# Attention, layer norm and feed-forward on one core: the first batch's weights rounded with one VectorE shift, sign and last bits made on ScalarE, differences on VectorE

## The chip, the cores and the metric

The kernel runs on one core of one Trainium2 chip. The metric is the device time of one launch in microseconds (us). Engines are called by the profile's names: PE (TensorE products), PEld (its weight loads), DVE (VectorE), ACT (ScalarE), POOL (GpSimd) and SP (SyncE, which here only issues transfers).

## The reference, cut to what matters

Four batches of causal attention (12 heads, 448 positions, head size 64), then a layer norm with gain and a feed-forward block with a residual. Shapes: `q`, `k`, `v` are (4, 12, 448, 64), the weights are 768 x 3072 and 3072 x 768.

```python
scores = scale * np.matmul(q, k.transpose(0, 1, 3, 2))   # masked above the diagonal
attn = softmax(scores)                                   # rows, max subtracted
x = np.matmul(attn, v)                                   # -> (4, 448, 768)
xn = (x - mu) / np.sqrt(var + 1e-06) * g_ln
out = x + np.maximum(xn @ w_ch1, 0.0) @ w_ch2
```

The scales in the set-up turn the inputs, the weights too, into float64, so a weight reaches the chip as two 32-bit words.

## The kernel before, in words

**Slots.** The feed-forward work of a batch is cut into 48 slots of 18 matrix products. Two slots use one weight unit of 128 x 1536, so a slot uses one half unit of 128 x 768. Slots 0 to 47 are batch 0, 48 to 95 batch 1, and so on. In each half of a batch 12 slots are products with `w1` (tile `ph`, L416) and 12 with `w2` (tile `po`, L435). Every float32 factor is split into two float32r parts whose sum it is: weights into `wh` and `wl`, activations into `xh`, `xl` and `hh`, `hl`. A product of 128 x 128 by 128 x 448 is three matmuls: high by high, low by high, high by low.

**Attention beside it.** While a batch's slots run, the attention of the next batch is worked on between them: one pair of heads in six slots, called a pair period here. Batch 0's own attention runs before slot 0, in slots with negative numbers (from about -50), with nothing beside it but the first four half units; batch 1's first pair of heads has its scores there too. The scores (`sc`, L229) get their mask and row minimum on DVE (L237), their exponentials on ACT (L251) and their scaling by `norm` (L267, tile `P` or `rest`), on POOL in batch 0 and on DVE in later batches; then PE transposes them (`pt`, L283), ACT or DVE evicts that (`PT`, L286 or L288), and PE multiplies by `v` (`px`, L298). In later batches DVE and POOL also make the parts of `q` and `k` (`qs` L195, `kl` L198).

**A half unit of the first batch.** `load_raw` brings in the float64 words (tile `raw`, five buffers), one slot's 128 x 768 at a time. Before the change, four instructions make the float32 weight, and two more split it:

- `convert1`: POOL multiplies the high word, read as a float32, by 0.0 and by 1.0 (L93, tile `z`: a zero with the weight's sign); ACT multiplies the same word by 2^-112 (L96, tile `w`), which puts the exponent where three shifts to the left make it float32's.
- `convert2`: DVE shifts the low word right by 29 and sets the sign bit into it (L101, `z`), then shifts `w` left by 3 and sets `z` into it (L105). The bits below float32's last place are cut off.
- `keep`: SP stores `w` in DRAM (L111, `scratch`), from where the three other batches load it (`full`).
- `split1`: ACT copies `w` to float32r (L116, `wh`); `split2`: `wl = w - wh` (L121), on POOL in the first batch, on DVE in the others.

**What sets the order.** Everything is issued in an order written out by the program, and each engine works through its own instructions in that order. In a slot first come the attention steps in `pre`, then the weight steps of `weights_ahead` (sorted: `split2`, `convert2`, `convert1`, `keep`, `load_raw`, `load_full`, `split1`), then the 18 products with their evictions (`hh` on ACT, L421, and `hl` on DVE, L422, or `xT` on DVE, L439), then the attention steps in `post`. From half unit 4 on, half unit s has `convert1` in slot s-4, `convert2` in s-3, `split1` in s-2 and `split2` in s-1. Half units 0 to 3 have them in the slots before 0, six slots apart.

Of the kernel before, what the change touches and what calls it, by code (L numbers as in the profile page):

```python
# [8 lines left out]
F32 = mybir.dt.float32  # L9
F32R = mybir.dt.float32r  # L10
U32 = mybir.dt.uint32
ACTF = mybir.ActivationFunctionType
ALU = mybir.AluOpType
PSUM = bass.MemoryType.PSUM
DRAM = bass.MemoryType.DRAM
# [4 lines left out]
P = 128  # L20
# [7 lines left out]
UH = UE // 2  # L28
# [11 lines left out]
ELAG = [2, 5, 7]  # L40
NDVE = 7
STATS = [(0, 3), (3, 5), (5, 6)]
OFF = [C * (i * (i + 1) // 2) for i in range(NC + 1)]


@with_exitstack
def kernel(ctx, tc, qk, v, w1, w2, g, out):
    nc = tc.nc

    def pool(name, bufs, **kw):  # L50
        return ctx.enter_context(tc.tile_pool(name=name, bufs=bufs, **kw))

    const = pool("const", 1)
    sb = pool("sb", 1)
# [5 lines left out]
    g_sb = const.tile([P, KC], F32, name="g_sb")  # L60
    mhalf = const.tile([C, NC], F32, name="mhalf")

# [1 line left out]
    # The first batch takes each unit from its float64 words, rounds it to float32 on the chip and  # L64
    # leaves it in DRAM for the other batches; every batch splits a unit into two float32r parts
    # whose sum is the float32.
    order = []
    for f0, f1 in ((0, HF), (HF, NF)):
        order += [("w1", f // 2) for f in range(f0, f1, 2)]
# [1 line left out]
    ns = 2 * len(order)  # L71
    scratch = [dr.tile([P, UE], F32, name=f"scratch{i}") for i in range(len(order))]
    ready = set()
    raw, zs, w32, wh, wl = {}, {}, {}, {}, {}

    def load_raw(s):
        kind, i = order[s // 2]
# [6 lines left out]
    def load_full(s):  # L84
        t = sb.tile([P, UE], F32, tag="raw", name="full", bufs=5)
        nc.sync.dma_start(out=t, in_=scratch[s % ns // 2])
        w32[s], w32[s + 1] = t[:, :UH], t[:, UH:]

    def convert1(s):
        high = raw[s][:, :, 1].bitcast(F32)  # L90
        zs[s] = sb.tile([P, UH], F32, tag="z", name="z", bufs=3)
        w32[s] = sb.tile([P, UH], F32, tag="w32", name="w32", bufs=4)
        nc.gpsimd.tensor_scalar(  # L93
            out=zs[s], in0=high, scalar1=0.0, scalar2=1.0, op0=ALU.mult, op1=ALU.mult
        )
        nc.scalar.activation(out=w32[s], in_=high, func=ACTF.Copy, scale=2.0 ** -112)  # L96

    def convert2(s):
        ready.add(s)
        z, w = zs.pop(s).bitcast(U32), w32[s].bitcast(U32)  # L100
        nc.vector.scalar_tensor_tensor(  # L101
            out=z, in0=raw.pop(s)[:, :, 0], scalar=29, in1=z,
            op0=ALU.logical_shift_right, op1=ALU.bitwise_or,
        )
        nc.vector.scalar_tensor_tensor(  # L105
            out=w, in0=w, scalar=3, in1=z, op0=ALU.logical_shift_left, op1=ALU.bitwise_or
        )

    def keep(s):
# [7 lines left out]

    def split2(s):
        wl[s] = sb.tile([P, UH], F32R, tag="wl", name="wl", bufs=4)
        eng = nc.gpsimd if s < ns else nc.vector  # L120
        eng.tensor_tensor(  # L121
            out=wl[s], in0=w32[s], in1=wh[s].bitcast(F32), op=ALU.subtract
        )

    def weights_ahead(start):
        """By slots, the work on the weights of later slots; the first halves of units are made
        ready while the first batch's attention runs."""
        early = 4
        todo = {}

        def put(t, *fs):
            todo.setdefault(max(t, start), []).extend(fs)

        for s in range(B * ns):
            t = (-EARLY + GAP * s, *ELAG) if s < early else (s - 4, 1, 2, 3)
            put(t[0] + t[3], (split2, s))
            if s < ns:
                put(t[0], (convert1, s))
                put(t[0] + t[1], (convert2, s))
                put(t[0] + t[1] + 1, (keep, s))  # L140
                if s + 5 < ns:
                    put(t[0] + t[1] + 1, (load_raw, s + 5))
            elif s % 2 == 0:
                put(s - 8, (load_full, s))
            put(t[0] + t[2], (split1, s))
        rank = [split2, convert2, convert1, keep, load_raw, load_full, split1]
        for fs in todo.values():
            fs.sort(key=lambda f: rank.index(f[0]))
        return todo

# [1 line left out]
    class Att:  # L152
        def __init__(self, b):
            self.b = b
# [45 lines left out]
        def scores(self, p, grp):  # L200
# [8 lines left out]
            for h, i in grp:  # L209
                n = C * (i + 1)  # L210
                if ("P", p, h) not in self.t:
                    x = 2 * p + h
                    if self.b == 0 and x % 5 >= 3:
                        a = 2 * NC * D * NP + (x % 5 - 3) * OFF[NC]
                        old = (x - 5) // 2, (x - 5) % 2
                        assert x < 5 or all(("T", *old, j) in self.done for j in range(NC))
                        self.t["P", p, h] = rest[:C, a:a + OFF[NC]]
                    else:
                        self.t["P", p, h] = sb.tile([C, OFF[NC]], F32, tag="P", name="P", bufs=3)
                if self.b == 0:  # L220
# [14 lines left out]
            for x, (h, i) in enumerate(grp):  # L235
                n = C * (i + 1)
                nc.vector.tensor_tensor_reduce(  # L237
                    out=self.t["P", p, h][:, OFF[i]:OFF[i + 1]], in0=pt[:, o:o + n],
                    in1=mask[:, S - n:], op0=ALU.add, op1=ALU.min, scale=-0.125, scalar=3.0e38,
# [5 lines left out]
        def exps(self, p, grp):  # L245
            nm = self.t.pop(("nm", p, tuple(grp)))
            for x, (h, i) in enumerate(grp):
                if ("sm", p, h) not in self.t:
                    self.t["sm", p, h] = sb.tile([C, NC], F32, tag="sm", name="sm", bufs=6)
                pp = self.t["P", p, h][:, OFF[i]:OFF[i + 1]]  # L250
                nc.scalar.activation(  # L251
# [5 lines left out]
        def norm(self, p, h):  # L257
# [7 lines left out]
            for i in (0, 1, 3, 2):  # L265
                pp = self.t["P", p, h][:, OFF[i]:OFF[i + 1]]
                eng.tensor_scalar(  # L267
# [37 lines left out]
        def stats(self, part, x):  # L305
            c0, c1 = STATS[part]
            assert all(("pv", c) in self.done for c in range(c0, c1))
            self.done.add(("stats", part, x))
            pt = ps.tile([C, S], F32, tag="pt", name="pln")
            for c in range(c0, c1):  # L310
                nc.tensor.transpose(  # L311
                    pt[:, (c - c0) * P:(c - c0 + 1) * P], self.xT[:, c, x * C:(x + 1) * C], ident
                )
            nc.vector.bn_stats(out=self.stat[:, x, part, :], in_=pt[:, :(c1 - c0) * P])
# [44 lines left out]
            )  # L359

        def steps(self):
            """The work by slots, relative to the first pair's: what goes before the products of
            the feed-forward layers in a slot, and what goes behind them."""
            pre, post = {}, {}

            def put(where, t, f, *a):
                where.setdefault(t, []).append((f, a))

            if self.b == 0:
                sat, tat, nat, end, ev = SAT0, TAT0, NAT0, END0, EV0  # L370
            else:
                sat, tat, nat, end, ev = SAT, TAT, NAT, END, EV1 if self.b == 1 else EV
            period = 6
            for p in range(NP):
                t0 = period * p
                if self.b:
                    put(pre, t0 - 4, self.load, p)
                    put(pre, t0 - 2, self.split1, p)
                    put(pre, t0 - 1, self.split2, p)
                for h in range(2):  # L380
                    put(pre, t0 + nat[h], self.norm, p, h)
                put(post, t0 + end, self.pv, p)
                for x, grp in enumerate(TGROUPS):
                    put(post, t0 + tat[x], self.transposes, p, grp, "act" if ev[x] else "dve")
                for x, grp in enumerate(SGROUPS):
                    put(post, t0 + sat[x], self.scores, p, grp)
                    put(pre, t0 + sat[x] + 1, self.exps, p, grp)
            tl = period * (NP - 1) + end + 1
            th = TH0 if self.b == 0 else TH
            for x in range(NC):  # L390
                put(post, th[0] + x, self.stats, 0, x)
                put(post, th[1] + x, self.stats, 1, x)
                put(post, tl + x // 2, self.stats, 2, x)
            ta = tl + NC // 2
            put(pre, ta, self.aggr)
            put(post, ta, self.spread)
            for c in range(KC):
                x = c if self.b else c // 2
                put(pre, ta + 1 + x, self.apply1, c)
                put(pre, ta + 1 + x + (self.b > 0), self.apply2, c)  # L400
            return pre, post, ta + (7 if self.b else 4)

# [1 line left out]
    def ffn(a, s, hh, hl):  # L404
        for f0, f1 in ((0, HF), (HF, NF)):
            for x in range(0, HF, 2):
# [38 lines left out]
    with tc.manual_schedule():  # L445
# [23 lines left out]
        for p in range(NP):  # L469
# [7 lines left out]
            out=mask[:, S - C:], in_=mask[:, S - C:], compare_op=ALU.is_ge, fill=-8.0e9,  # L477
# [3 lines left out]
        for s in range(4, 5):  # L481
            pre.setdefault(start + 6 + 4 * s, []).append((load_raw, (s,)))
        feed, ahead = None, weights_ahead(start)
        for s in range(start, B * ns):
            for b in range(1, B):
# [6 lines left out]
            if s >= 0:  # L492
# [3 lines left out]
                if s % ns == 0:  # L496
                    feed = ffn(att[s // ns], s, hh, hl)
# [38 lines left out]
```

## Time and profile before

| what | value |
|---|---|
| median of 3 runs | 960.81 us (958.25 to 961.01) |
| span of the profiled execution | 955.6 us |
| that execution's own time | not listed apart from its span; the median is 5.2 us above the span |
| PE busy | 908.6 us (95%) |
| PEld busy | 794.1 us (83%) |
| DVE busy | 626.7 us (66%) |
| ACT busy | 416.8 us (44%) |
| POOL busy | 283.1 us (30%) |

The span runs from the first to the last instruction. Busy time is the time in which an engine works at least on one instruction; an instruction that is held up by another engine counts as busy as long as it is held. Percentages are means over stages that differ, so the stages are looked at one by one below.

### The profile page before, as it was taken

What the parts mean: (1) busy time and instruction counts of PE and PEld (TensorE: products, weight loads), DVE (VectorE), ACT (ScalarE), POOL (GpSimd) and SP (SyncE); (2) the same over time, 40 slices, a digit from 0 to 9 for tenths busy, and PEclk for the clock granted to TensorE, in tenths of its full rate; (3) what the DMA queues carried; (4) which work ended last, traced back from release to release, by engine and by line L of the source; (5) the groups of instructions that cost most, each with busy time, mean ns of one, the idle gap of its engine ahead of it and who ended that gap; (6) DMA issues with size and microseconds to landing.
All of it is one profiled execution on the core that took longest, in us unless ns stands there. A gap on an engine that the chain in (4) does not pass through costs nothing.

```text
span 955.6 us, 13000 instructions
## 1 busy us (share of the span) xinstructions
PE 908.6 (95%) x4864; PEld 794.1 (83%) x4864; DVE 626.7 (66%) x1208; ACT 416.8 (44%) x859; POOL 283.1 (30%) x211
## 2 busy tenths in 40 slices
PE   6888988998998799999999999999999999999998
PEld 4556877887787698898888998898888999999997
DVE  5978999999989746656565566666665544333432
ACT  6754565547553344444543245443443233323320
POOL 7654675887758901111010311110010210000000
PEclk9988998999999999999999999999999999999999
DMA  9730667767677654332322463323322243233310
GB/s 252 270 112 1 213 232 270 250 221 278 217 249 239 234 192 147 115 135 80 134 80 76 150 226 115 139 87 137 115 100 76 98 165 116 100 103 119 108 56 36
DMA packets 35246, 144.36 MB, mean 151 GB/s; under 512 B 4080, under 2 KB 8688, under 8 KB 35184
## 3 DMA queue, kind: packets, MB, share of 16 engines
q1 hardware_dynamic: 35184, 143.54, 43.5%
q8 instruction: 38, 0.62, 0.3%
q14 instruction: 24, 0.20, 0.1%
HBM read 119.15 MB, written 24.38 MB: 150 GB/s over the span
## 4 chain that ended last, share of the span: by engine, by line
PE 65%; POOL 0%; DVE 0%; ACT 0%; issue 0%; POOLq 0%; ACTq 0%
PE po L435 29%; PE ph L416 28%; PE sc L229 3%; PE px L298 3%; PE pt L283 2%; PE pln L311 1%; POOL wl L121 0%; PE rb L336 0%; PE mb L331 0%; DVE w L105 0%; ACT wh L116 0%; DVE xT L439 0%; POOL xl L356 0%; POOLq L121 0%; ACTq L116 0%
## 5 line engine op out<-in xcount | busy, mean ns | idle before, releaser
L435 PE MATMUL po<-hh,wl 128*128 128x448 f32 x576 | 212.7, 369 | 8.7 <-POOL wl L121 8.7
L416 PE MATMUL ph<-xh,wh 128*128 128x448 f32 x576 | 215.2, 374 | 3.4 <-DVE hl L422 2.0
L435 PE MATMUL po<-hh,wh 128*128 128x448 f32 x576 | 215.6, 374 | 0.0
L416 PE MATMUL ph<-xl,wh 128*128 128x448 f32 x576 | 212.1, 368 | 0.5 <-POOL xl L356 0.5
L416 PE MATMUL ph<-xh,wl 128*128 128x448 f32 x576 | 211.4, 367 | 1.0 <-POOL wl L121 1.0
L435 PE MATMUL po<-hl,wh 128*128 128x448 f32 x576 | 212.0, 368 | 0.0
L422 DVE SCALAR_TENSOR_TENSOR hl<-ph,hh 128x448 fp32r<-128x448 f32 x96 | 59.7, 622 | 128.1 <-ACT hh L421 128.1
L116 ACT ACTIVATE wh<-full 128x768 fp32r<-128x768 f32 x144 | 119.5, 839 | 54.8 <-PE po L435 50.8
L121 DVE TENSOR_TENSOR wl<-full,wh 128x768 fp32r<-128x768 f32 x144 | 136.3, 953 | 0.8 <-ACT wh L116 0.5
L198 POOL TENSOR_TENSOR kl<-qkraw,kh 128x896 fp32r<-128x896 f32 x18 | 48.2, 2678 | 278.8 <-DVE kh L188 267.3
L251 ACT ACTIVATE P<-P,nm 112x448 f32<-112x448 f32 (+3 forms) x176 | 91.7, 522 | 81.9 <-DVE nm L237 77.9
L435 PEld LDWEIGHTS po<-hh,wl 128*128 128x128 f32 x576 | 109.2, 190 | 20.4 <-POOL wl L121 11.6
L421 ACT ACTIVATE hh<-ph 128x448 fp32r<-128x448 f32 x96 | 51.9, 540 | 162.8 <-PE ph L416 162.7
L416 PEld LDWEIGHTS ph<-xh,wh 128*128 128x128 f32 x576 | 109.2, 190 | 13.0 <-DVE hl L422 2.3
L416 PEld LDWEIGHTS ph<-xh,wl 128*128 128x128 f32 x576 | 108.9, 189 | 10.3 <-POOL wl L121 1.7
L435 PEld LDWEIGHTS po<-hh,wh 128*128 128x128 f32 x576 | 109.4, 190 | 8.5
L416 PEld LDWEIGHTS ph<-xl,wh 128*128 128x128 f32 x576 | 109.1, 189 | 8.8 <-POOL xl L356 0.9
L435 PEld LDWEIGHTS po<-hl,wh 128*128 128x128 f32 x576 | 109.3, 190 | 8.2
L121 POOL TENSOR_TENSOR wl<-w,wh 128x768 fp32r<-128x768 f32 x48 | 103.2, 2151 | 36.8 <-issue 15.2
L439 DVE TENSOR_TENSOR xT<-po,xT 128x448 f32<-128x448 f32 x48 | 29.9, 622 | 115.6 <-PE po L435 115.6
L237 DVE CUSTOM_DVE_ANT_0 P<-sc,mask 112x448 f32<-112x448 f32 (+3 forms) x176 | 70.2, 443 | 38.2 <-PE sc L229 26.6
L105 DVE SCALAR_TENSOR_TENSOR w<-w,z 128x768 uint32<-128x768 uint32 x48 | 90.0, 1875 | 3.1
(64 smaller groups left out, 1049.0 us busy)
## 6 DMA issues: line engine op xcount, KB each, us to landing
full<-scratch SPq DMA_DIRECT2D x72, 768.0 KB, 4.2
raw<-w_dram SPq DMA_DIRECT2D x48, 768.0 KB, 4.9
scratch<-w SPq DMA_DIRECT2D x48, 384.0 KB, 2.7
qkraw<-qk_dram SPq DMA_DIRECT2D x18, 896.0 KB, 7.2
out_dram<-xT SPq DMA_DIRECT2D x24, 224.0 KB, 2.0
vt<-v_dram SPq DMA_DIRECT2D x18, 224.0 KB, 5.6
first_qk<-qk_dram SPq DMA_DIRECT2D x8, 224.0 KB, 5.3
rest<-v_dram SPq DMA_DIRECT2D x6, 224.0 KB, 7.4
```

Of the source, the lines that this page charges most:

```text
L105: nc.vector.scalar_tensor_tensor(out=w, in0=w, scalar=3, in1=z, op0=ALU.logical_shift_left, op1=ALU.bitwise_or)
L116: nc.scalar.activation(out=wh[s], in_=w32[s], func=ACTF.Copy)
L121: eng.tensor_tensor(out=wl[s], in0=w32[s], in1=wh[s].bitcast(F32), op=ALU.subtract)
L198: nc.gpsimd.tensor_tensor(out=kl, in0=rk, in1=kh.bitcast(F32), op=ALU.subtract)
L229: nc.tensor.matmul(pt[:, o:o + n], lhsT=qs[:, h, C * i:C * i + C], rhs=kk[:, h, :n], start=(part == 0), stop=(part == 1),)
L237: nc.vector.tensor_tensor_reduce(out=self.t["P", p, h][:, OFF[i]:OFF[i + 1]], in0=pt[:, o:o + n], in1=mask[:, S - n:], op0=ALU.add, op1=AL ...
L251: nc.scalar.activation(out=pp, in_=pp, func=ACTF.Exp, scale=-1.0, bias=nm[:, x:x + 1], accum_out=self.t["sm", p, h][:, i:i + 1],)
L416: nc.tensor.matmul(pm[y], lhsT=w[:, c * P:c * P + P], rhs=z[:, c, :], start=(c == 0 and i == 0), stop=(c == KC - 1 and i == 2),)
L421: nc.scalar.activation(out=hh[:, x + y, :], in_=pm[y], func=ACTF.Relu)
L422: nc.vector.scalar_tensor_tensor(out=hl[:, x + y, :], in0=pm[y], scalar=0.0, in1=hh[:, x + y, :].bitcast(F32), op0=ALU.max, op1=ALU.subtract,)
L435: nc.tensor.matmul(pm, lhsT=w[:, o:o + P], rhs=z[:, x, :], start=(x == 0 and i == 0), stop=(x == HF - 1 and i == 2),)
L439: nc.vector.tensor_tensor(out=a.xT[:, m, :], in0=pm, in1=a.xT[:, m, :], op=ALU.add)
```

## The change: what it does, and the diff

The sign no longer has a tile of its own. ACT's multiplication becomes a two-sided one (Prelu): a positive high word is multiplied by 2^-112, a negative one by 2^-80, which sets the bit that the shift by three moves into the sign's place. A second ACT instruction turns the low word, a whole number, into the last bits: times 239/256 x 2^-29, converted to a whole number (tile `bits`), which rounds where the shift cut off. DVE is left with one instruction, the shift of `w` with `bits` set into it. `split2` is on DVE in the first batch too. POOL has no weight work any more.

```diff
+LAST = 239 / 256
...
     def convert1(s):
-        high = raw[s][:, :, 1].bitcast(F32)
-        zs[s] = sb.tile([P, UH], F32, tag="z", name="z", bufs=3)
+        bits[s] = sb.tile([P, UH], U32, tag="bits", name="bits", bufs=3)
         w32[s] = sb.tile([P, UH], F32, tag="w32", name="w32", bufs=4)
-        nc.gpsimd.tensor_scalar(
-            out=zs[s], in0=high, scalar1=0.0, scalar2=1.0, op0=ALU.mult, op1=ALU.mult
+        nc.scalar.activation(
+            out=w32[s], in_=raw[s][:, :, 1].bitcast(F32), func=ACTF.Prelu, scale=2.0 ** -112,
+            alpha=2.0 ** 32,
         )
-        nc.scalar.activation(out=w32[s], in_=high, func=ACTF.Copy, scale=2.0 ** -112)
+        nc.scalar.activation(
+            out=bits[s], in_=raw.pop(s)[:, :, 0], func=ACTF.Copy, scale=LAST * 2.0 ** -29
+        )
...
     def convert2(s):
         ready.add(s)
-        z, w = zs.pop(s).bitcast(U32), w32[s].bitcast(U32)
+        w = w32[s].bitcast(U32)
         nc.vector.scalar_tensor_tensor(
-            out=z, in0=raw.pop(s)[:, :, 0], scalar=29, in1=z,
-            op0=ALU.logical_shift_right, op1=ALU.bitwise_or,
-        )
-        nc.vector.scalar_tensor_tensor(
-            out=w, in0=w, scalar=3, in1=z, op0=ALU.logical_shift_left, op1=ALU.bitwise_or
+            out=w, in0=w, scalar=3, in1=bits.pop(s), op0=ALU.logical_shift_left,
+            op1=ALU.bitwise_or,
         )
...
     def split2(s):
         wl[s] = sb.tile([P, UH], F32R, tag="wl", name="wl", bufs=4)
-        eng = nc.gpsimd if s < ns else nc.vector
-        eng.tensor_tensor(
+        nc.vector.tensor_tensor(
             out=wl[s], in0=w32[s], in1=wh[s].bitcast(F32), op=ALU.subtract
         )
```

**DVE, in a pair period of batch 0's slots, before.** The rows go from the end of one slot (its eviction `hl`) over the scaling of a head and the copy `kh` to the next slot's eviction. The numbers behind `w` are the half unit's.

```order
L422 SCALAR_TENSOR_TENSOR hl<-ph,hh 128x448
L262 TENSOR_SCALAR r<-sm 112x4
L263 RECIPROCAL r<-r 112x4
L267 TENSOR_SCALAR P<-P,r 112x112
...
L188 CAST kh<-qkraw 128x896
L101 SCALAR_TENSOR_TENSOR z<-raw,z 128x768
L105 SCALAR_TENSOR_TENSOR w_1293<-w_1293,z 128x768
L422 SCALAR_TENSOR_TENSOR hl<-ph,hh 128x448
L195 TENSOR_TENSOR qs<-qkraw,qs 64x896
```

The same stretch of the changed program:

```order
L427 SCALAR_TENSOR_TENSOR hl<-ph,hh 128x448
L267 TENSOR_SCALAR r<-sm 112x4
L268 RECIPROCAL r<-r 112x4
L272 TENSOR_SCALAR P<-P,r 112x112
...
L193 CAST kh<-qkraw 128x896
L126 TENSOR_TENSOR wl<-w_1177,wh 128x768
L110 SCALAR_TENSOR_TENSOR w_1282<-w_1282,bits 128x768
L427 SCALAR_TENSOR_TENSOR hl<-ph,hh 128x448
L200 TENSOR_TENSOR qs<-qkraw,qs 64x896
```

DVE still has two weight instructions in a slot: the shift that made `z` has gone, and in its place, one earlier, stands the difference `wl` of the half unit two steps ahead in its making.

**ACT, the same pair period's end, before and in the changed program** (`P,sm` are the exponentials, `PT` the evicted transposes):

```order
L251 ACTIVATE P,sm<-P,nm 112x112
L251 ACTIVATE P,sm<-P,nm 112x336
L96 ACTIVATE w_1610<-raw 128x768
L116 ACTIVATE wh<-w_1506 128x768
L286 COPY PT<-pt 112x448
```

```order
L256 ACTIVATE P,sm<-P,nm 112x112
L256 ACTIVATE P,sm<-P,nm 112x336
L99 ACTIVATE w_1593<-raw 128x768
L103 ACTIVATE bits<-raw 128x768
L122 ACTIVATE wh<-w_1491 128x768
L291 COPY PT<-pt 112x448
```

One instruction more stands between the exponentials and `wh`. In both programs ACT has one table load, at its beginning.

**POOL, at the first slots of batch 0, before and in the changed program** (`xl` belongs to the layer norm of batch 0, `kl` to batch 1's heads):

```order
L356 TENSOR_TENSOR xl<-xg,xh 128x448 x6
L93 TENSOR_SCALAR z<-raw 128x768 x3
L198 TENSOR_TENSOR kl<-qkraw,kh 128x896
L121 TENSOR_TENSOR wl<-w_939,wh 128x768
L93 TENSOR_SCALAR z<-raw 128x768
```

```order
L361 TENSOR_TENSOR xl<-xg,xh 128x448 x6
L203 TENSOR_TENSOR kl<-qkraw,kh 128x896
```

Behind it, POOL's next instruction in the changed program is the `kl` of the next pair of heads. The orders of PE and of SP are the same in both programs.

## Rows read from the trace of the kernel before

**Rows 1.** The page's busy tenths in 40 slices of the span.

```profile
PE   6888988998998799999999999999999999999998
DVE  5978999999989746656565566666665544333432
```

**Rows 2.** Busy time by stage: slots 0 to 47, slots 48 to 95, one pair period.

```profile
core 0: us, PE busy (x) PEld busy (x) DVE busy (x) ACT busy (x) POOL busy (x), PEclk, DMA share, GB/s
84.20:339.70 255.50, 230.05 (x1201) 198.81 (x1202) 233.80 (x325) 134.90 (x252) 190.07 (x107) 0.96 0.66 228
339.70:558.10 218.40, 218.40 (x1218) 195.62 (x1217) 133.86 (x311) 92.75 (x198) 25.29 (x13) 1.00 0.36 125
...
114.60:148.10 33.50, 30.81 (x169) 26.32 (x168) 31.39 (x50) 20.18 (x41) 24.23 (x14) 1.00 0.70 246
```

**Rows 3.** The chain that ended last: start, duration, what.

```profile
324.84 2.49 POOL wl L121
327.37 12.36 PE po L435 x52
...
347.05 0.91 PE sc L229 x6
...
351.62 0.81 PE sc L229 x6
...
356.08 0.51 PE sc L229 x4
...
375.24 1.10 PE sc L229 x6
```

**Rows 4.** PE's waits, 84 to 340 us: total, times, longest.

```profile
PE pt L283 <- DVE P L267: 13.1, 11, 2.5
PE po L435 <- POOL wl L121: 8.7, 7, 1.9
```

**Rows 5.** DVE in order of time: start, duration.

```profile
207.70 2.42 DVE L105 SCALAR_TENSOR_TENSOR w<-w,z 128x768 uint32<-128x768 uint32 x1
```

**Rows 6.** POOL over the same stretch, 199 to 214 us.

```profile
206.76 2.54 POOL L121 TENSOR_TENSOR wl<-w,wh 128x768 fp32r<-128x768 f32 x1
```

**Rows 7.** Durations by tile, ns: least, median, most.

```profile
L101 DVE SCALAR_TENSOR_TENSOR z<-raw,z x48: 935/1122/4452, 15.3 to 324.3; 128x768 uint32<-128x768 uint32 x48
L105 DVE SCALAR_TENSOR_TENSOR w<-w,z x48: 957/1625/6049, 16.5 to 325.7; 128x768 uint32<-128x768 uint32 x48
L121 DVE TENSOR_TENSOR wl<-full,wh x144: 941/950/1336, 333.8 to 945.2; 128x768 fp32r<-128x768 f32 x144
L96 ACT ACTIVATE w<-raw x48: 869/899/933, 14.3 to 320.4; 128x768 f32<-128x768 f32 x48
L198 POOL TENSOR_TENSOR kl<-qkraw,kh x18: 2067/2712/2786, 54.8 to 696.9; 128x896 fp32r<-128x896 f32 x18
L195 DVE TENSOR_TENSOR qs<-qkraw,qs x18: 1089/1242/4120, 53.7 to 699.3; 64x896 fp32r<-64x896 f32 x18
```

**Rows 8.** DVE's groups in the pair period: busy us, mean ns, idle before.

```profile
L105 DVE SCALAR_TENSOR_TENSOR w<-w,z 128x768 uint32<-128x768 uint32 x6 | 12.2, 2028 | 0.2
L101 DVE SCALAR_TENSOR_TENSOR z<-raw,z 128x768 uint32<-128x768 uint32 x6 | 7.0, 1169 | 0.0
```

**Rows 9.** DVE and POOL before slot 0, each in order of time.

```profile
23.01 4.45 DVE L101 SCALAR_TENSOR_TENSOR z<-raw,z 128x768 uint32<-128x768 uint32 x1
...
22.93 1.95 POOL L267 TENSOR_SCALAR rest<-rest,r 112x112 f32<-112x112 f32 x4
24.80 1.84 POOL L121 TENSOR_TENSOR wl<-w,wh 128x768 fp32r<-128x768 f32 x1
```

**Rows 10.** PE's waits over the whole span.

```profile
PE pt L283 <- DVE PT L288: 6.4, 3, 3.0
```

**Rows 11.** Groups of the whole span: xl on POOL, the table load on ACT.

```profile
L356 POOL TENSOR_TENSOR xl<-xg,xh 128x448 fp32r<-128x448 f32 x24 | 32.2, 1341 | 39.1 <-ACT xh L353 38.7
...
L251 ACT ACT_TABLE_LOAD x1 | 1.3, 1283 | 0.7 <-PEq L525 0.7
```

More of the change, by code (lines that the diff above doesn't have):

```diff
@@ L73 @@
     ready = set()
-    raw, zs, w32, wh, wl = {}, {}, {}, {}, {}
+    raw, bits, w32, wh, wl = {}, {}, {}, {}, {}
     def load_raw(s):
```

## The prediction

> **What bounds the kernel now.** First the busy slices of the page [rows 1]: for the first third of the span DVE stands at 9 in nearly every slice and PE moves between 6 and 9; after that PE stands at 9 and DVE falls to 7 and less. So there are two kernels here, and the changed instructions are all in the first one. Second the chain of waits [rows 3]: from 327.37 us to the end it is PE alone, product after product; the last hand-over from other engines is a `wl` that POOL made for slot 46. Behind slot 48 (339.7 us) nothing but PE counts, and no instruction there is changed. Third the busy time by stage [rows 2]: slots 0 to 47 take 255.5 us, slots 48 to 95 take 218.4 us, and in the latter PE is busy for all 218.40. Both run the same PE instructions, but for the scores of batch 1's first pair, which the earlier stage has behind it: 0.91 + 0.81 + 0.51 = 2.2 us [rows 3]. So PE could do the first batch in 216.2 us, and 255.5 - 216.2 = **39.3 us** are lost there. 25.5 us of them are idle (255.5 - 230.05 busy); the rest is PE being slower: the granted clock is 0.96 there and 1.00 in the stage behind [rows 2], that is, part of the stage ran at 1.2 instead of 2.4 GHz, and PE had been waiting in between. PE's waits name scaled scores from DVE, 13.1 us, and `wl` from POOL, 8.7 us [rows 4].
>
> Why is DVE late? Its shifts take 1.9 and 1.4 us on average, but 0.96 and 0.94 at best [rows 7]. The long ones lie over POOL's work: a `w` that begins at 207.70 takes 2.42 us [rows 5] and ends just behind POOL's `wl`, which runs from 206.76 to 209.30 [rows 6]. Before slot 0 it is plainer: a `z` that begins at 23.01 takes 4.45 us, to 27.46 [rows 9]; POOL scales from 22.93 and makes a `wl` until 26.64, and 0.8 us later the shift is done. So DVE instructions with two inputs in SBUF and POOL's work hold each other up, and the sum of both is what the first batch pays.
>
> **The change part by part.** I take a pair period (six slots) as the unit: 33.5 us before [rows 2]; its floor on PE is 375.24 - 347.05 = 28.2 us, two like points of batch 2's attention in the chain [rows 3].
>
> *DVE.* Of its 31.39 us in the period [rows 2], `z` (7.0) and the slow `w` (12.2) go [rows 8]. In come six shifts at the 0.96 of an undisturbed one, 5.7 us, and six `wl` at the 0.95 that the later batches' `wl` take, 5.7 us [rows 7]. `qs`, which lies over `kl` and `wl`, can go from 2.1 to 1.1 us [rows 7], 1.0 us. Sum: 31.4 - 7.0 - 12.2 + 5.7 + 5.7 - 1.0 = 22.6 us. POOL keeps one `kl` of 2.07 to 2.71 us a period [rows 7], which can hold DVE for as long: at most 25.3 us, under 28.2.
>
> *ACT.* 20.18 us [rows 2] plus six `bits`. The trace has no such conversion from whole numbers to whole numbers. Below: 0.87 us, the least of the `w` that reads the same tile with the same step [rows 7]; above, three times that row's median, 2.7 us, if the conversion took several passes. I take the median, 0.90: it is the nearest row in tile, size and engine. Prelu in place of Copy I cost at nothing, same engine, tile and size, and keep 0.1 us of each `w` for the range. ACT then has 20.2 + 5.4 = 25.6 of 28.2 us. That is tight, and in single slots with three exponentials ACT will be behind PE; but what it makes is used one slot later or more.
>
> The Trainium skill (ScalarE: Activation LUTs, Rules for kernel authors) speaks against this part: it wants multiplications on VectorE and not on ScalarE. By that rule the second shift would stay on DVE, and the sum there would be 22.6 + 5.7 = 28.3, with `kl` up to 31.0 us in the period, over PE's 28.2. The rows make the two prices alike, 0.94 us on DVE at best and 0.90 on ACT [rows 7], and only ACT has the room.
>
> *POOL* loses 96 instructions and has 2 to 3 us of work in a period. `kl` goes up its queue, past the `wl` and `z` that stood around it. *SP* and the DMAs are unchanged; `raw` is given back by ACT instead of DVE, a slot earlier.
>
> *The new wait.* DVE's `wl` waits for ACT's `wh`, and behind it in DVE's queue stand a shift and then `hl`, for which PE's next product tile waits. ACT issues that `wh` one slot ahead, so this costs nothing as long as ACT stays within a slot of PE; the cover is that slot, some 4.7 us.
>
> *Slots 0 to 47.* 39.3 us are to be had. I leave 2 us for the first slot, where PE starts from a pause at the lower clock, and 5 us for slots in which DVE or ACT is late: below 0, as in slots 48 to 95, where the same `kl` and `xl` disturb DVE and PE never waits [rows 2]; above, every `kl` (six of 2.07) and every `xl` (six of 1.34, [rows 11]) in full, 20.4 us. 5 is nearer to the lower end, since DVE has room for a `kl` in a period. Gain 39.3 - 7 = **32.3 us**.
>
> *Before slot 0.* Three `z` are of the 4.45 kind. DVE's own saving: before 1.1 + 3 x 4.45 + 4 x 0.96 = 18.3 us at most [rows 7, 9]; now eight instructions of 0.95, 7.6 us, each half of them (`wl`, at a scaling on POOL) perhaps held for one scaling group, 1.95 us [rows 9]: 7.6 to 15.4. That frees 3 to 11 us of DVE, of which PE waited 6.4 us for `PT` evictions behind such a `z` [rows 10]. ACT's four `bits`, 3.6 us, I take as hidden, since DVE is the full engine there [rows 1]; without that cover they would eat up the gain. I take **3.5 us**, about half of PE's wait, range 0 to 11.
>
> Sum: 32.3 + 3.5 = 35.8 us. Taken from the profiled span, 955.6 us, this leaves 919.8; the median stands 5.2 us above that span, so 960.8 - 35.8 = **925.0 us**. Its own bounds: 39.3 - 2 - 0 + 11 = 48 at best (913), 39.3 - 22.4 + 0 = 17 at worst (944).
>
> **The rivals.** *DVE stays the bound (12%).* If the slow `w` were slow by itself and not through POOL, the period would be 31.4 - 7.0 + 5.7 = 30.1 us, 1.9 over PE, six periods long: 925 + 11 = 936. Against it: the same instruction takes 0.96 in other slots [rows 7].
>
> *ACT becomes the bound (10%).* With `bits` at 1.9 us, what a whole-number instruction averaged on DVE, ACT has 20.2 + 6 x 1.9 = 31.6 us: 3.4 over PE in six periods, 925 + 20 = 945. For it: ACT is the fullest engine behind PE in my own sum.
>
> *Slower (3%).* The same place, the upper bound: from (33.5 - 20.2) / 6 = 2.2 us for a `bits` on, ACT's period is longer than all of 33.5. At 2.7 us it is 36.4, 8.2 over PE in six periods (49 us), and in the twelve slots without much attention ACT would need some 5 us against 3.7 (15 us): 925 + 64 = 989. Against it: every row of ACT over 128 x 768 is between 0.82 and 0.93.
>
> *Tables (1%).* If Prelu and Exp needed different tables, ACT would load one each time they alternate: three groups of exponentials in a period, each between two conversions, six loads of 1.28 us [rows 11], ACT at 25.6 + 7.7 = 33.3, 5.1 over PE, 925 + 31 = 956, and some 3 us more before slot 0: about no change. Against it: the order of the changed program has one table load. The Trainium skill (ScalarE: Activation LUTs, Table sets) has such loads for functions of different sets, and does not list Prelu among those that every set has; with its 2.66 us a switch the period would be 41.6 us and the time about 1005 us. The one load in the order speaks against it either way.
>
> **How the numbers follow.** The forecast, PE as the bound of the first batch, has 74%, and the four rivals 12, 10, 3 and 1%. The range 912 to 945 holds the forecast's own bounds, DVE as the bound, and ACT as the bound just at its edge; outside are the slow `bits`, the tables and the tails, about 15%. A measurement of this kernel can tell 0.3% (2.9 us) from no change. Faster by more than that: 74 + 12 + 10 less a little for what I have not seen, 95%; within it 2%; slower 3%.
>
> **What the profile of the changed kernel would show.** Right: slots 0 to 47 in some 223 us with PE's granted clock near 1.00; `w` on DVE near 0.96 us with no long ones but beside `kl` or a scaling; DVE's share of that stage from 92% to about 80%, ACT's from 53% to about 80%; the chain PE alone from soon behind slot 0; from slot 48 to the end of the span 615.9 us as before (955.6 - 339.7). Wrong: `bits` well over 0.9 us, ACT busy over 95% with PE waiting for `hh`, `wh` or exponentials through it, more than one table load; or DVE still full with `w` over 1.5 us.

## The result, and the profile after

The changed kernel takes **918.88 us** (median of 4 runs, 918.60 to 920.24) against 959.53 us for the kernel before (4 runs): a ratio of 0.958, 95% interval 0.957 to 0.960, or 40.7 us less. The forecast was 925.0 us, range 912 to 945. One more launch of the changed kernel, among the five that ran for number 9 below, took 2443 us; why is open, and it is in no median here. From profiled span to profiled span the step is 955.6 - 918.4 = 37.2 us; the forecast for this was 35.8.

Slot 0 begins at 79.2 instead of 84.2 us, slot 48 at 302.6 instead of 339.7. The busy tenths of the slices, which answer to [rows 1]:

```profile
PE   6988999999999999999999999999999999999998
DVE  4877678777778566655664676556664634333431
```

PE is at 9 from the fifth slice on, and DVE reaches 8 in three slices only. Busy time by stage (stretch, its length, then PE, PEld, DVE, ACT and POOL busy, PE's granted clock, DMA share, GB/s), which answers to [rows 2]: before slot 0, slots 0 to 47, slots 48 to 95; then one pair period, from one `xT` that ACT evicts to the next, and the first 5.8 us of slot 0.

```profile
0.00:79.20 79.20, 63.99 (x369) 42.29 (x369) 51.88 (x179) 51.90 (x147) 37.25 (x71) 0.96 0.63 191
79.20:302.60 223.40, 221.09 (x1201) 194.48 (x1202) 170.88 (x325) 167.47 (x296) 35.07 (x19) 0.99 0.75 260
302.60:521.00 218.40, 218.40 (x1218) 195.64 (x1217) 134.55 (x311) 93.19 (x199) 26.79 (x14) 1.00 0.36 126
...
105.50:135.45 29.95, 29.49 (x161) 24.92 (x162) 22.93 (x48) 24.79 (x48) 3.60 (x1) 1.00 0.75 257
...
79.20:85.00 5.80, 5.03 (x16) 4.31 (x17) 5.66 (x10) 2.53 (x5) 5.47 (x5) 0.71 0.00 0
```

Slots 0 to 47 fell from 255.5 to 223.4 us, of which PE could do them in 216.2. The 39.3 us that were lost there have become 7.2. They shrank on two counts: PE's idle time from 25.5 to 2.3 us (223.40 - 221.09), and its busy time over 216.2 from 13.9 to 4.9 us, with the granted clock at 0.99 instead of 0.96: where PE no longer stops, it stays at the upper of its two levels, 2.4 GHz. Of the 7.2 us, 2.7 are slot 0: it takes 6.4 us (79.2 to 85.5) against 3.7 for a slot without a wait, with the granted clock at 0.71 in its first 5.8 us. DVE went from 234 to 171 us in the stage (76% of it), ACT from 135 to 167 (75%), POOL from 190 to 35. From slot 48 on nothing changed.

Durations in ns (least/median/most) by tile, which answer to [rows 7]:

```profile
L99 ACT ACTIVATE w<-raw x48: 886/901/962, 15.0 to 287.8; 128x768 f32<-128x768 f32 x48
L110 DVE SCALAR_TENSOR_TENSOR w<-w,bits x48: 947/953/1941, 16.8 to 291.3; 128x768 uint32<-128x768 uint32 x48
L126 DVE TENSOR_TENSOR wl<-w,wh x48: 926/951/959, 24.3 to 295.9; 128x768 fp32r<-128x768 f32 x48
...
L103 ACT ACTIVATE bits<-raw x48: 870/900/947, 15.8 to 288.6; 128x768 uint32<-128x768 uint32 x48
...
L200 DVE TENSOR_TENSOR qs<-qkraw,qs x18: 1087/1241/4048, 47.3 to 662.2; 64x896 fp32r<-64x896 f32 x18
...
L203 POOL TENSOR_TENSOR kl<-qkraw,kh x18: 2077/2716/3601, 48.3 to 659.8; 128x896 fp32r<-128x896 f32 x18
```

The shift on DVE has gone from a median of 1.63 to 0.95 us with the same size and types, and the difference takes 0.95 where POOL took 2.09 (median). ACT's Prelu costs what the Copy cost, 0.90, and so does `bits`. PE's waits in the stage, 79 to 303 us (total, times, longest), against [rows 4]:

```profile
PE ph L421 <- ACT xh L358: 1.4, 1, 1.4
PE ph L421 <- DVE hl L427: 0.9, 1, 0.9
PE ph L421 <- POOL xl L361: 0.8, 1, 0.8
PE pt L288 <- DVE P L272: 0.4, 1, 0.4
```

The wait for `wl` (8.7 us) has gone, and of the one for scaled scores (13.1 us) 0.4 us are left.

### The profile page after: what moved, and what is told of

Same layout as the page of the kernel before. It is cut to its first block, busy times and chain, and to the rows that moved or that the text cites. A ratio compares the mean times of both kernels' runs of the same rounds, so it can differ in the third digit from the quotient of the medians.

```text
span 918.4 us, 12826 instructions
## 1 busy us (share of the span) xinstructions
PE 897.3 (98%) x4864; PEld 790.0 (86%) x4864; DVE 554.0 (60%) x1208; ACT 452.8 (49%) x907; POOL 121.6 (13%) x115
## 4 chain that ended last, share of the span: by engine, by line
PE 87%; ACT 6%; DVE 5%; DMA 1%; issue 1%; SPq 1%; POOL 0%; ACTq 0%
PE po L440 38%; PE ph L421 33%; PE px L303 5%; PE sc L234 4%; PE pt L288 4%; ACT P L256 2%; PE pln L316 1%; DMA raw<-w_dram 1%; ACT w L99 1%; ACT bits L103 1%; PE sc L227 1%; DVE hl L427 1%; ACT wh L122 1%; DVE P L272 1%; DVE wl L126 1%
## 5 line engine op out<-in xcount | busy, mean ns | idle before, releaser
L203 POOL TENSOR_TENSOR kl<-qkraw,kh 128x896 fp32r<-128x896 f32 x18 | 51.8, 2877 | 378.5 <-DVE kh L193 378.5
L288 PE MATMUL pt<-ident,P 112*112 112x112 f32 x440 | 55.3, 262 | 4.1 <-ACT PT L291 3.0
L288 PEld LDWEIGHTS pt<-ident,P 112*112 112x112 f32 x440 | 47.1, 134 | 13.9 <-ACT PT L291 4.6
```

What stands on the lines that cost most here:

```text
L203: nc.gpsimd.tensor_tensor(out=kl, in0=rk, in1=kh.bitcast(F32), op=ALU.subtract)
L288: nc.tensor.transpose(pt[:, o:o + C], pp[:, a:a + C], ident[:C, :C])
```

## The experiments

The question after the result: did the time come from DVE and POOL no longer holding each other up (the theory), or from `wl` no longer coming late from POOL (the rival)? And is ACT really the place with room? The first four kernels ran on one chip with 7 runs of the kernel before, 960.1 us in the median; the next four on one chip, 961.0; the last three on one chip, 960.1.

**1. The difference back on POOL.**

```diff
     def split2(s):
-        nc.vector.tensor_tensor(
+        eng = nc.gpsimd if s < ns else nc.vector
+        eng.tensor_tensor(
```

> The changed kernel with the difference wl of the first batch back on POOL (sign by Prelu and last bits on ACT stay). Holding theory (DVE and POOL instructions that meet hold each other up, and DVE was full): DVE loses z (7.0 us of 31.4 in a pair period) and has 24.4 or less, under PE's 28.2, so most of the gain stays: 920 to 932 us, with some w near 2.4 us over POOL's wl. Rival (what counted was that POOL's wl came late to PE): the wait for wl stays, and the time is nearer to before, 940 to 955 us.

Measured: 923.97 us, ratio 0.963 (0.960 to 0.965). So 36 of the 41 us are there with `wl` still on POOL. PE's waits for it are 1.9 us in this kernel:

```profile
PE ph L422 <- POOL wl L127: 1.5, 2, 0.8
...
PE po L441 <- POOL wl L127: 0.4, 1, 0.4
```

POOL was late before because DVE was late with `w`, from which ACT makes the `wh` that `wl` needs. In slots 0 to 47 of the kernel before ACT waited for `w`:

```profile
ACT wh L116 <- DVE w L105: 32.1, 14, 4.1
```

With `z` gone ACT hardly waits for `w`, and POOL stands ready for `wh` 19 times:

```profile
ACT wh L122 <- DVE w L110: 0.7, 1, 0.7
...
POOL wl L127 <- ACT wh L122: 65.8, 19, 6.2
```

So POOL is in time though its `wl` still takes 1.86 us (median). The rival falls. Of the change's parts, moving `wl` is worth 5 us and taking `z` off DVE and POOL the rest, in this order of doing them; done first, moving `wl` is worth 16 us (number 2).

**2. Only the difference moved.** The kernel before with the diff's last part alone, `split2` on VectorE for all half units.

```diff
     def split2(s):
-        eng = nc.gpsimd if s < ns else nc.vector
-        eng.tensor_tensor(
+        nc.vector.tensor_tensor(
```

> The kernel before with one part of the change alone: wl of the first batch on DVE, z on POOL and both shifts on DVE as before. Holding theory: DVE has three weight instructions of 0.95 us in a slot, 31.4 - 7.0 - 12.2 + 17.2 - 1.0 = 28.4 us in a pair period, and up to 5.2 us more where it meets POOL's z: 28.4 to 33.6, so 930 to 958 us, best guess 941, with DVE still over 90% busy in slots 0 to 47. Rival (lateness of POOL's wl): with wl on DVE the lateness is gone, 920 to 928 us.

Measured: 943.81 us, ratio 0.983 (0.980 to 0.987). DVE has a third weight instruction in each slot and the kernel is still 16 us faster, since POOL's longest one has gone. DVE's groups in slots 0 to 47 (busy us, mean ns, idle before):

```profile
L105 DVE SCALAR_TENSOR_TENSOR w<-w,z 128x768 uint32<-128x768 uint32 x44 | 54.6, 1240 | 1.6
L120 DVE TENSOR_TENSOR wl<-w,wh 128x768 fp32r<-128x768 f32 x44 | 47.9, 1089 | 0.1
L101 DVE SCALAR_TENSOR_TENSOR z<-raw,z 128x768 uint32<-128x768 uint32 x44 | 47.7, 1084 | 0.0
```

Here DVE is the bound, with 227.5 of 244.4 us busy, and PE waits 13.7 us for `wl`, now DVE's: lateness follows the engine that is full.

```profile
PE po L434 <- DVE wl L120: 8.9, 5, 2.3
PE ph L415 <- DVE wl L120: 4.8, 4, 2.1
```

**3. POOL's work put back, for nobody.** Nothing waits for these results; the computation is the changed kernel's. What can still be waited for are the buffers: POOL has to have read `raw`, `w` and `wh` before they are filled again, and `bits` has two buffers instead of three.

```diff
     def convert1(s):
-        bits[s] = sb.tile([P, UH], U32, tag="bits", name="bits", bufs=3)
+        bits[s] = sb.tile([P, UH], U32, tag="bits", name="bits", bufs=2)
...
+        nc.gpsimd.tensor_scalar(
+            out=sb.tile([P, UH], F32, tag="spare", name="spare", bufs=1),
+            in0=raw[s][:, :, 1].bitcast(F32), scalar1=0.0, scalar2=1.0, op0=ALU.mult, op1=ALU.mult,
+        )
...
     def split2(s):
...
+        if s < ns:
+            nc.gpsimd.tensor_tensor(
+                out=sb.tile([P, UH], F32, tag="spare", name="spare", bufs=1),
+                in0=w32[s], in1=wh[s].bitcast(F32), op=ALU.subtract,
+            )
```

> The changed kernel with POOL's two weight instructions of before run again into a tile that nobody reads (so nothing waits for their results; bits has two buffers instead of three to make room). Holding theory: DVE's w and wl are held up by POOL as w and z were; DVE is back at about 31 us or more in a pair period, and the time goes most of the way back, 945 to 962 us, with a mean w or wl of 1.4 us or more. Rival (lateness of POOL's wl, or fewer instructions in the chain): nothing on PE's way changed, 918 to 924 us.

Measured: 947.74 us, ratio 0.987 (0.984 to 0.990): 29 of the 41 us are lost again. DVE's groups in slots 0 to 47, and beside them POOL and DVE around 140 us:

```profile
L130 DVE TENSOR_TENSOR wl<-w,wh 128x768 fp32r<-128x768 f32 x44 | 63.9, 1453 | 0.1
L114 DVE SCALAR_TENSOR_TENSOR w<-w,bits 128x768 uint32<-128x768 uint32 x44 | 61.7, 1403 | 0.0
```

```profile
140.37 2.44 POOL L134 TENSOR_TENSOR spare<-w,wh 128x768 f32<-128x768 f32 x1
142.90 1.65 POOL L103 TENSOR_SCALAR spare<-raw 128x768 f32<-128x768 f32 x1
...
142.85 0.95 DVE L130 TENSOR_TENSOR wl<-w,wh 128x768 fp32r<-128x768 f32 x1
143.72 1.64 DVE L114 SCALAR_TENSOR_TENSOR w<-w,bits 128x768 uint32<-128x768 uint32 x1
```

`wl` and POOL's spare begin together at 142.9; `wl` runs through in 0.95, POOL's takes 1.65 instead of its least, 0.88; then DVE's `w` takes 1.64, to 145.4. Three instructions that by themselves take 0.95, 0.88 and 0.95 fill 2.5 us on two engines: they run nearly one after the other. The buffers are the smaller part, ACT's waits for them in slots 0 to 47 being these:

```profile
ACT w L99 <- POOL spare L134: 2.7, 2, 1.4
ACT bits L107 <- DVE w L114: 2.4, 4, 0.6
```

So by these waits some 5 of the 29 us at most are theirs, and the rest is the holding by itself, with no result of POOL's on anybody's way. The other 12 of the 41 us are not told apart; before, POOL's results were waited for, and here they are not.

**4. ACT's new instruction twice.**

```diff
+        nc.scalar.activation(
+            out=bits[s], in_=raw[s][:, :, 0], func=ACTF.Copy, scale=LAST * 2.0 ** -29
+        )
         nc.scalar.activation(
             out=bits[s], in_=raw.pop(s)[:, :, 0], func=ACTF.Copy, scale=LAST * 2.0 ** -29
         )
```

> The changed kernel with the ACT instruction that makes bits issued twice (same result). ACT had 23.4 of 28.5 us in a pair period of the changed kernel; six more of 0.90 make 28.8. If ACT has the room that the prediction gave it, this is at the edge: 919 to 928 us. If ACT was already what holds PE, each of the 44 copies costs its 0.9 us: 950 us or more.

Measured: 936.57 us, ratio 0.975 (0.972 to 0.978): 17.7 us more than the changed kernel, between the two expectations. The four copies before slot 0 are paid in full: it begins at 82.9 instead of 79.2 us. The 44 copies in slots 0 to 47 are 39.6 us, of which 13.4 are paid (236.8 against 223.4 us), a third. Slots 0 to 47, and the wait of DVE's `hl` there:

```profile
82.90:319.70 236.80, 227.97 (x1201) 197.58 (x1202) 170.30 (x325) 205.74 (x340) 36.39 (x19) 0.97 0.72 246
```

```profile
DVE hl L430 <- ACT hh L429: 43.5, 22, 3.2
```

ACT is busy for 87% of the stage only, and yet PE is idle for 8.8 us, its granted clock is down to 0.97 and its busy time up by 6.9. PE's waits name DVE (scaled scores 4.3 us, `hl` 1.9, `wl` 1.2), but DVE's work is that of the changed kernel; its `hl` waits 43.5 us for ACT's `hh`, 26.6 in the changed kernel. The expectation's 23.4 of 28.5 us come from a stretch 1.4 us short of a period, which leaves out a part of its exponentials; over a whole period it is 24.8 of 29.95 (above), and with six more of 0.90 it is 30.2: no room at all. A sum over a period that just fits is not room either: a slot in which ACT is late stops PE, and a stop costs the clock as well.

**5. The last bits on DVE.** A shift of the low word by 29 that cuts off, in place of ACT's conversion (the last place of the weights is cut instead of rounded).

```diff
-        nc.scalar.activation(
-            out=bits[s], in_=raw.pop(s)[:, :, 0], func=ACTF.Copy, scale=LAST * 2.0 ** -29
-        )
...
     def convert2(s):
...
+        nc.vector.tensor_scalar(
+            out=bits[s], in0=raw.pop(s)[:, :, 0], scalar1=29, scalar2=None,
+            op0=ALU.logical_shift_right,
+        )
```

> The changed kernel with the last bits made on DVE by a shift of the low word right by 29 (cut off instead of rounded), no bits instruction on ACT. A shift with one input and a step of two words has no row yet; at 0.94 us, as the z shift at best, DVE has 21.5 + 5.6 = 27.1 us in a pair period of 28.5, plus what kl holds. Theory (the place is chosen by which engine has room, and ACT at 23.4 has more than DVE would): 922 to 932 us, PE waiting for wl or hl here and there. If VectorE is the better place, as the Trainium skill's rule for multiplications would have it (ScalarE: Activation LUTs, Rules for kernel authors), ACT's 5.5 us less in a period show and the time is below 918.

Measured: 922.13 us (921.1 to 922.8), ratio 0.960 (0.958 to 0.963). The shift with one input takes 0.55 us, much less than the 0.94 that I put in:

```profile
L107 DVE TENSOR_SCALAR bits<-raw x48: 547/553/1541, 14.0 to 292.6; 128x768 uint32<-128x768 uint32 x48
```

```profile
75.90:303.40 227.50, 221.09 (x1201) 194.12 (x1202) 197.63 (x369) 135.43 (x252) 32.73 (x19) 0.99 0.73 255
```

The Trainium skill (ScalarE: Activation LUTs, Rules for kernel authors) wants multiplications on VectorE and not on ScalarE. For the price of the instruction this run agrees, with 0.55 us for a shift on VectorE in place of 0.90 for the multiplication on ScalarE. The start profits: slot 0 is at 75.9 instead of 79.2 us. But slots 0 to 47 take 227.5 instead of 223.4 us, with PE waiting 5.4 us for `wl`. In that stage the place with room counts more than the price.

**6. `kl` on DVE,** the holding that the change left.

```diff
-            nc.gpsimd.tensor_tensor(out=kl, in0=rk, in1=kh.bitcast(F32), op=ALU.subtract)
+            nc.vector.tensor_tensor(out=kl, in0=rk, in1=kh.bitcast(F32), op=ALU.subtract)
```

> The changed kernel with kl (batches 1 to 3) on DVE instead of POOL. What is left of the holding is kl against qs: qs takes 2.4 us in a pair period and 4.05 once before slot 0, with PE then waiting 2.4 us for an eviction. Holding theory: qs falls to 1.09 us and kl costs DVE about 1.1, so DVE's sum stays, the slots at the pair's end shorten by some tenths and the 2.4 us go: 914 to 917.5 us. If the remaining losses are ACT's, 918 to 920 us.

Measured: 917.02 us, ratio 0.955 (0.953 to 0.958), and once more below. `qs` and `kl`, one behind the other on DVE, take 1.09 us each, where in the changed kernel they lay over each other and took 1.09 to 4.05 and 2.08 to 3.60:

```profile
L200 DVE TENSOR_TENSOR qs<-qkraw,qs x18: 1087/1089/1457, 44.8 to 658.1; 64x896 fp32r<-64x896 f32 x18
...
L203 DVE TENSOR_TENSOR kl<-qkraw,kh x18: 1091/1092/1322, 46.3 to 659.2; 128x896 fp32r<-128x896 f32 x18
```

The gain is before slot 0 (it begins at 75.0 us). Slots 0 to 47 take 223.4 us as they did: there the holding by `kl` was covered, as the prediction had it.

**7 and 8. The first conversions two slots later,** alone and with `kl` on DVE.

```diff
-EARLY = 45
+EARLY = 43
```

> The changed kernel with the first four conversions two slots later (EARLY 43 instead of 45). The chain before slot 0 has ACT waiting 2.1 us for the first raw words with exponentials and evictions behind it (PE waits 3.0 us for one), and wl meets the scaling on POOL. If that head of the queue is what costs: 915 to 917.5 us. If the start is bound by other things: 918 to 920 us.

> Both edits together, kl on DVE and the first conversions two slots later: 911 to 916 us if both gains stand and add up, 918 to 920 us if neither does.

Measured: 923.47 us (ratio 0.961, 0.959 to 0.964) and 919.84 us (0.958, 0.955 to 0.961). Number 7 is above both of its ranges and number 8 misses the gain, for two reasons. ACT's wait for the first words goes, but slot 0 is no earlier: 79.3 us in number 7 against 79.2 in the changed kernel, 75.7 in number 8 against 75.0 in number 6. And PE is slower from slot 48 to the end. The first two of the last four half batches in the chain of number 7:

```profile
741.61 44.16 PE ph L421 x216
785.76 44.16 PE po L440 x216
```

In the changed kernel, as in the kernel before and in every other one, these take 43.77 to 43.93 us, with PE's instructions, tiles and waits the same in the program; it adds up to 2.9 us from slot 48 on in number 7 and 2.8 in number 8. Numbers 5 and 6, on the same chip, do not show it. Why is open; it was not followed further.

**9. A faster version, beside the changed kernel.** The last three ran together: the changed kernel, number 6, and number 6 with the last bits of the first four half units cut off by a shift on DVE.

```diff
+        if s < 4:
+            nc.vector.tensor_scalar(
+                out=bits[s], in0=raw.pop(s)[:, :, 0], scalar1=29, scalar2=None,
+                op0=ALU.logical_shift_right,
+            )
```

> The changed kernel itself once more, so that the next two stand beside it on the same chip: 918 to 921 us.

> The changed kernel with kl on DVE once more, beside the changed kernel on the same chip. If its gain of some 2 us stands: 916 to 918 us, below the changed kernel's lowest run; if it was chance: the same as the changed kernel.

> kl on DVE, and for the four half units made before slot 0 the last bits are made by a shift on DVE (cut off, 0.55 us) instead of on ACT. Before slot 0 the chain of the kernel with kl on DVE runs through ACT, exponential after exponential, with the first conversions in between. Theory (ACT is the bound there now): four times 0.83 us go from the chain, slot 0 begins at about 72 instead of 75.0 us, and the time is 913 to 915.5 us. If other engines bind there: no change, 916 to 918 us.

Measured: 919.54 us (median of 4; ratio 0.958, 0.955 to 0.960), 916.33 us (0.954, 0.952 to 0.957) and **915.65 us** (0.953, 0.950 to 0.955). Number 6 stands, 916.0 to 917.6 in its runs against 918.9 and more. The last one's runs, 913.6 to 916.0, end where number 6's begin. It gained less than expected: slot 0 is at 75.0 us, where number 6 had it at 76.6 on this chip and at 75.0 on the other, so the 0.7 us between the medians are the most that can be claimed, and the runs of the two touch. The chain before slot 0 no longer runs through the later three of ACT's conversions there, but through a transfer:

```profile
34.73 9.42 DMA qkraw<-qk_dram
```

## Why the prediction was right, point by point

- **The bound.** "PE could do the first batch in 216.2 us" and 7 us more: forecast 223.2, measured 223.4. The 32.3 us of that step were 32.1. This was the step that carried the forecast, and it holds. Its two terms hold too: 2 us for slot 0 were 2.7, and 5 us for late slots were 4.5. A small misreading: the last hand-over to PE, at 327.37 us, is the `wl` of slot 45, not 46.
- **Holding as the cause.** Number 3 shows it with POOL's work alone, number 1 shows that the late `wl` was a consequence. The rival "DVE stays the bound" has fallen: `w` is at 0.95 in the median. How the two engines hold each other up is argued from the durations; that they do is shown.
- **DVE's sum,** 22.6 to 25.3 us in a pair period: 22.9. One term in it was wrong: `qs` was to fall to 1.1 us and stayed at 2.4 beside `kl`. It cost nothing in the slots, and 2.4 us of waiting once before slot 0.
- **ACT's sum,** 25.6 us in a pair period: 24.8, since instructions that follow each other closely overlap (a `bits` of 0.90 us begins 0.80 us after its `w`) and the busy time counts that once. The period itself is 28.4 to 30.0 us long in the changed kernel, against a floor of 28.2. `bits` at 0.90 and Prelu at nothing were right. But "that is tight" was truer than the price I gave it: number 4 shows that 0.9 us more in a slot is no longer free. The rival "ACT becomes the bound" did not come, and was nearer than 10% sounds.
- **The new wait,** `wl` on DVE for ACT's `wh`: never in the first batch, and once, for 0.5 us, in the later ones. The cover of one slot held.
- **Before slot 0:** 3.5 us forecast, 5.0 measured, within 0 to 11. The `z` of 4.45 us have no follower: the longest `w` there is 1.9 us. DVE's saving there is 10.5 us (62.40 busy to 51.88), at the upper end of the 3 to 11 forecast. But the step "ACT's four `bits` I take as hidden" did not hold. In the changed kernel three of the four stand in the chain before slot 0, two of them here:

```profile
33.00 0.83 ACT bits L103
...
41.18 0.83 ACT bits L103
```

Issued twice they put slot 0 off by 3.7 us (number 4), and taken off ACT they brought it forward by 3.3 (number 5); two profiles of one kernel differ by up to 1.6 us there. So the term came near its forecast in part because two errors worked against each other, which is luck. With `kl` off POOL another chain is as long, and taking the four conversions off ACT gave 0.7 us at most (number 9).
- **From the span to the median** is the step that missed most: I added the 5.2 us by which the median of before stood over its profiled span. The kernel before takes 2.1 us around its own span (957.71 us with a span of 955.6 is one of its runs), so some 3.1 of the 5.2 were that its profiled execution was one of its quickest. The changed kernel takes 1.8 us around its span (920.24 - 918.4), and its profiled execution was the slowest of its four, 1.4 us above the median. Of the 6.1 us between forecast and result 4.7 are this step, and 1.4 the span.
- **The rivals on the other side,** slow conversions and table loads: no `bits` over 0.95 us, and Prelu beside Exp ran without another load.

## What to carry to other kernels

Where VectorE is full, look first at what GpSimd does beside it. Here an instruction whose duration varied between once and several times its least, over GpSimd's work, was being held, and GpSimd's work alone cost the kernel up to 29 us. Here the engine with room in the slot was the better place than the one with the cheapest instruction, and it needed more than a few per cent of room: with ACT at 87%, 6.5 us more of idle TensorE came with 6.9 us more of busy time at a lower granted clock. And take the sum against the span, with the overhead between span and time known, before it is set beside a median.

## What the runs showed of the hardware that was not expected

- A whole-number shift on DVE with one input in SBUF takes 0.55 us over 128 x 768 with a step of two words, one with two inputs 0.95.
- An ACT conversion from whole numbers to whole numbers, with a scale, costs what a copy costs, 0.90 us over 128 x 768, and a two-sided scale (Prelu) as much.
- Not only DVE instructions with two tiles as inputs got longer over POOL's work. With it put back (number 3), the scaling of 112 x 112 went from 0.30 to 0.47 us in the mean and the small sum in front of the reciprocal (`r` from `sm`, 112 x 4) from 0.18 to 0.33, while the reciprocal stayed at 0.18 and the `PT` copies at 0.62.
- PE's pace at the upper clock differed by 0.5 to 0.9% between programs with the same PE instructions (44.16 against 43.77 and 43.93 us for 216 products), in the profiles of numbers 7 and 8 against all others. The cause is open.
